# Retention and SwiGLU kernel: a second joined attention visit in two down-projections, and the loads placed to match

## The chip, the cores and the metric

The kernel runs on one core of one Trainium2 chip. The metric is the device time of one execution in microseconds (us). The engines named below are TensorE (PE, with its weight loads as PEld), VectorE (DVE), ScalarE (ACT), GpSimd (POOL) and SyncE (SP), which issues transfers.

## The reference

A retention layer (linear attention with a decaying state) feeds a feed-forward layer.

```python
# q, k, v: (batch 4, heads 8, seq 768, head_dim 64)
gamma = 1.0 - 2.0 ** (-5.0 - np.arange(H))
for t in range(S):
    state = gamma * state + einsum('bhd,bhe->bhde', k[:, :, t], v[:, :, t])
    y[:, :, t] = scale * einsum('bhd,bhde->bhe', q[:, :, t], state)
# x: y with its heads side by side, 3072 tokens x 512
xn = x / sqrt(mean(x * x) + 1e-6) * rms_g
out = (silu(xn @ w_gate) * (xn @ w_val)) @ w_out     # 512 -> 1536 -> 512
```

## The kernel before, in words

**Chunks and units.** The 768 positions are cut into six chunks of 128. A chunk holds four units, one for each batch; units 0 and 1 are pair 0, units 2 and 3 are pair 1, so a pair is 256 tokens and a chunk is 512. `(d, b)` below is unit `b` of chunk `d`; `(d, p)` after `values` or `a_pair` is a pair.

**Attention of a chunk.** `load` brings q, k and v of a unit from memory by three transfers that GpSimd issues (q and k are cast to bf16 on the way). `vp` scales v by the decay on GpSimd. `t_dma` transposes q and k into `qT` and `kT` by two transfers that SP issues. `a_pair` computes q-k products of a pair (`a_ps`, line 488): for each unit into two PSUM banks. `a_mask` (DVE, line 497) applies the causal mask and copies them out as `am`. `values` computes for a pair the products of `am` and `vp` (line 517), the k-v products for the state (`kv_ps`, line 526, not in the last chunk) and the product of `qT` and the old state `st_b` (line 534). `y_out` (DVE) scales the result into `x`, `state_add` (DVE) adds `kv_ps` to the state, `state_cast` (POOL) recasts it to bf16. Then `square` (ACT) and `rstd` (POOL) give the norm's factor, `norm` (DVE) writes `xn`, and `x_dma` (SP) transposes it into `xnT`, which `begin` has set up.

**Feed-forward of a chunk.** `gv` computes gate and value products of one or two of the twelve 128-column blocks of the hidden layer (lines 563, `g_ps` and `v_ps`), ACT applies silu (`sg`) and DVE multiplies (`hT`). `down` multiplies one unit's `hT` by `w_out` (line 584), ACT copies the result out (`o_sb`) and SP stores it. In the loop at the end of the kernel the first four `gv` steps of a chunk take 256 tokens and two blocks each, so the first two need pair 0 of `xnT` and the next two pair 1; eight steps with 512 tokens and one block follow.

**Order.** The order on every engine is the order of the program; nothing is moved by a scheduler. From chunk 1 on the feed-forward of chunk `c` is a list of 16 steps (0 to 11 `gv`, 12 to 15 `down`), and the attention of chunk `d = c + 1` is threaded between them: `after[n]` lists what is issued behind step `n`. In the loop at the end of the kernel `c` runs from 2 to 5. A stretch of attention work on TensorE between two steps is called a visit here.

A joined visit is a call such as `values(d, 1, (d + 1, 0), True)`: the values of pair 1 of chunk `d` are followed at once by the q-k products of pair 0 of the next chunk. The last argument puts the values' PSUM tiles into the banks of the feed-forward (four, taken in turn), while the q-k products take the other four. Before, each of the steps 11 of `c` = 2 and `c` = 3 (and no other) carries such a visit.

**Queues and buffers.** Transfers on one queue are issued in the program's order, and an issue that waits for its data holds up all that stand behind it on that engine: a `t_dma` on SP waits for its load to land, and `x_dma` and the stores of `down` share SP with it. On GpSimd the loads share the order with `vp`, `rstd` and `state_cast`. All transfers run on the same 16 DMA engines. There are six buffers for `v`, eight each for `q`, `k`, `qT`, `kT` and `vp`, and twelve for `am`.

Of the kernel before, what the change touches and what calls it, by code (L numbers as in the profile page):

```python
# [16 lines left out]
def kernel(  # L17
# [16 lines left out]
    NCH = S // C  # L34
# [716 lines left out]
    def run(steps, after):  # L751
        for i, step in enumerate(steps):
            MARK[i] = step()
            for f in after.get(i, ()):
                f()

    def L(f, *a):
        return lambda: f(*a)
# [20 lines left out]
        12: [L(values, 2, 1), L(load, 3, 2, "qkv", 12),  # L779
             L(y_out, 2, 1, 0), L(y_out, 2, 1, 1), L(square, 2, 1, 0), L(square, 2, 1, 1), L(rstd, 2, 1),  # L780
             L(state_add, 2, 1), L(norm, 2, 1, 0, 1), L(x_dma, 2, 1, 0), L(x_dma, 2, 1, 1),
             L(state_cast, 1), L(vp, 3, 0), L(load, 3, 3), L(vp, 3, 1), L(t_dma, 3, 2)],
        14: [L(t_dma, 3, 3)],
    })

    for c in range(2, NCH):

        steps = [L(gv, c, n, n + 2, t, t + 256) for t in (0, 256) for n in (0, 2)]
        steps += [L(gv, c, n, n + 1, 0, GT) for n in range(4, NFF)]
        steps += [L(down_last if (c, b) == (NCH - 1, B - 1) else down, c, b) for b in range(B)]  # L790
        d = c + 1
        more = d + 1 < NCH
        after = {}
        if d == 3:
            after = {
                0: [L(begin, d)],
                1: [L(a_pair, d, 0), L(a_mask, d, 0, 0)],
                2: [L(a_mask, d, 0, 1), L(a_mask, d, 1, 0)],
                3: [L(a_mask, d, 1, 1), L(load, d + 1, 0)],
                4: [L(values, d, 0), L(vp, d, 2), L(vp, d, 3)],  # L800
                5: [L(y_out, d, 0, 0), L(y_out, d, 0, 1), L(state_add, d, 0), L(load, d + 1, 1)],
                6: [L(square, d, 0, 0), L(square, d, 0, 1), L(rstd, d, 0), L(t_dma, d + 1, 0)],
                7: [L(a_pair, d, 1), L(a_mask, d, 2, 0), L(state_cast, 0)],
                8: [L(a_mask, d, 2, 1), L(a_mask, d, 3, 0), L(t_dma, d + 1, 1), L(vp, d + 1, 0), L(load, d + 1, 2)],
                9: [L(a_mask, d, 3, 1), L(norm, d, 0, 0), L(x_dma, d, 0, 0), L(vp, d + 1, 1)],
                10: [L(norm, d, 0, 1), L(x_dma, d, 0, 1), L(load, d + 1, 3)],
            }
        elif d < NCH:
            after = {
                0: [L(begin, d)],  # L810
                1: [L(values, d, 0)] + [L(load, d + 1, 0)] * more,
                2: [L(y_out, d, 0, 0), L(vp, d, 2), L(vp, d, 3)],
                3: [L(y_out, d, 0, 1)] + [L(state_add, d, 0), L(load, d + 1, 1)] * more,
                4: [L(square, d, 0, 0)],
                5: [L(a_pair, d, 1), L(a_mask, d, 2, 0), L(square, d, 0, 1), L(rstd, d, 0)]
                   + [L(state_cast, 0), L(t_dma, d + 1, 0)] * more,
                6: [L(t_dma, d + 1, 1), L(load, d + 1, 2)] * more + [L(a_mask, d, 2, 1), L(norm, d, 0, 0), L(x_dma, d, 0, 0)],
                7: [L(norm, d, 0, 1), L(x_dma, d, 0, 1), L(a_mask, d, 3, 0)] + [L(vp, d + 1, 0)] * more,
                8: [L(a_mask, d, 3, 1)] + [L(load, d + 1, 3), L(vp, d + 1, 1)] * more,
            }  # L820
        if d < NCH:
            if more:
                after.update({
                    11: [L(values, d, 1, (d + 1, 0), True), L(y_out, d, 1, 0), L(y_out, d, 1, 1),
                         L(square, d, 1, 0), L(square, d, 1, 1), L(rstd, d, 1), L(state_add, d, 1),
                         L(a_mask, d + 1, 0, 0), L(a_mask, d + 1, 0, 1), L(norm, d, 1, 0, 1), L(x_dma, d, 1, 0)],
                    12: [L(x_dma, d, 1, 1), L(a_mask, d + 1, 1, 0, 1), L(state_cast, 1), L(t_dma, d + 1, 2)],
                    13: [L(t_dma, d + 1, 3)],
                })
            else:  # L830
                after.update({
                    9: [L(values, d, 1)],
                    10: [L(y_out, d, 1, 0)],
                    11: [L(y_out, d, 1, 1), L(square, d, 1, 0), L(square, d, 1, 1), L(rstd, d, 1)],
                    12: [L(norm, d, 1, 0, 1), L(x_dma, d, 1, 0), L(x_dma, d, 1, 1)],
                })
        run(steps, after)
# [1 line left out]
_INS = ['q', 'k', 'v', 'moe_w_gate', 'moe_w_val', 'moe_w_out', 'moe_rms_g']  # L839
# [26 lines left out]
```

## Time and profile before

| | |
|---|---|
| median of 5 runs | 238.81 us (237.41 to 239.49) |
| the profiled execution: its own time | 240.91 us |
| its span, first to last instruction | 238.9 us |
| mean granted TensorE clock | 0.993 of full speed |
| busy: DVE, ACT, POOL | 127.1, 87.6, 118.3 us |
| gate and value products (line 563) | 76.0 and 75.8 us |
| down-projections (lines 584 and 598) | 61.1 and 2.8 us |
| loads and weights on GpSimd's queue | 17.04 MB, 72.6% of the DMA engines' time |
| SP's queue: transposes, stores | 13.25 MB, 33.5% of it |

The profile covers one execution. The busy time of an engine is the union of its instructions' spans; the mean duration of a single matmul is longer than its share of the busy time, because matmuls are pipelined. The two queues' shares add up to over 100% because packets of several queues overlap on an engine. The chain of waits follows the work that ended last back to what released it, step by step. In the lists in order of time, a row has start, length, engine, line, operation, and the number of instructions merged into it. A transfer's time to landing counts from its issue.

### The profile page before, as it was taken

To read this page: it belongs to the slowest core of one execution; us is meant where nothing else is said; L and a number is where in the kernel's file an instruction comes from. 1 tells how busy PE (TensorE), PEld (TensorE's weight loads), DVE (VectorE), ACT (ScalarE), POOL (GpSimd) and SP (SyncE) were. 2 spreads that over 40 slices of the span, in tenths; PEclk is the share of its full clock that TensorE was granted. 3 is DMA by queue.
4 is the path that set the end of the run, shared out by engine and by line. 5 is a ranking of instruction groups with operands and counts; after the bars stand their busy time and mean duration, and the time that the engine had idled before them with its cause. 6 is when DMAs were issued, how large, how long until landed. Compare 5 with 4: busy or idle time off the path is not lost.

```text
span 238.9 us, 5561 instructions
## 1 busy us (share of the span) xinstructions
PE 227.8 (95%) x2290; PEld 138.6 (58%) x2290; DVE 127.1 (53%) x222; ACT 87.6 (37%) x176; POOL 118.3 (50%) x154
## 2 busy tenths in 40 slices
PE   6887999999999999599999999999999999999994
PEld 2455775546888854485454585454684544864443
DVE  3775545826577784145798037868145842234300
ACT  2965634233432423122524225314235242333211
POOL 8966799589598839960595901937001001000000
PEclk9999999999999999889999999999999999999999
DMA  8999999999999999999999999891640204200022
GB/s 101 166 184 203 188 181 172 194 200 211 169 164 137 142 159 133 180 243 172 73 108 112 187 192 200 87 135 27 172 113 0 47 0 130 93 0 0 0 92 88
DMA packets 87467, 30.78 MB, mean 129 GB/s; under 512 B 73681, under 2 KB 83153, under 8 KB 87442
## 3 DMA queue, kind: packets, MB, share of 16 engines
q0 software_dynamic: 55488, 17.04, 72.6%
q1 hardware_dynamic: 31280, 13.25, 33.5%
q8 instruction: 18, 0.29, 0.6%
q10 hardware_dynamic: 674, 0.14, 0.3%
q14 instruction: 7, 0.06, 0.1%
HBM read 29.36 MB, written 6.29 MB: 149 GB/s over the span
## 4 chain that ended last, share of the span: by engine, by line
PE 82%; DMA 9%; DVE 4%; issue 2%; POOL 2%; DVEq 0%; POOLq 0%
PE g_ps L563 25%; PE v_ps L563 24%; PE o_ps L584 22%; DMA xnT<-xn 3%; DMA wv_b<-in_moe_w_val_dram 3%; DMA k2b<-in_k_dram 2%; PE a_ps L488 2%; PE y_ps L517 2%; DVE am L290 1%; PE y_ps L534 1%; PE o_ps L598 1%; PE kv_ps L526 1%; DVE hT L568 1%; PE a_ps L283 1%; DVE am L497 1%
## 5 line engine op out<-in xcount | busy, mean ns | idle before, releaser
L568 DVE TENSOR_TENSOR hT<-sg,v_ps 128x512 bf16<-128x512 bf16 (+1 forms) x76 | 49.9, 657 | 78.1 <-PE v_ps L563 74.4
L563 PE MATMUL g_ps<-xnT,wg_b 128*128 128x256 bf16 (+1 forms) x428 | 76.0, 313 | 3.4 <-DMA xnT<-xn 2.5
L563 PE MATMUL v_ps<-xnT,wv_b 128*128 128x256 bf16 (+1 forms) x428 | 75.8, 312 | 0.9 <-DMA wv_b<-in_moe_w_val_dram 0.7
L567 ACT ACTIVATE sg<-g_ps 128x512 bf16<-128x512 f32 (+1 forms) x76 | 43.7, 575 | 78.3 <-PE g_ps L563 78.1
L584 PE MATMUL o_ps<-wo_b,hT 128*128 128x512 bf16 x276 | 61.1, 379 | 0.0
L563 PEld LDWEIGHTS <-wv_b 128*128 128x128 bf16 x428 | 42.0, 99 | 22.8 <-DMA wv_b<-in_moe_w_val_dram 1.7
L563 PEld LDWEIGHTS <-wg_b 128*128 128x128 bf16 x428 | 40.7, 99 | 24.6 <-issue 3.6
L584 PEld LDWEIGHTS <-hT 128*128 128x128 bf16 x276 | 26.5, 98 | 31.4
L457 POOL TENSOR_SCALAR m<-ms 128x2 f32<-128x2 f32 x10 | 2.2, 218 | 61.9 <-ACT xsq L452 61.9
L588 ACT COPY o_sb<-o_ps 128x512 f32<-128x512 f32 x23 | 13.4, 584 | 43.7 <-PE o_ps L584 36.1
L465 DVE SCALAR_TENSOR_TENSOR xn<-x,rstd,g_bc 128x512 bf16<-128x512 f32 x20 | 19.2, 987 | 9.8 <-POOL rstd L373 9.8
L497 DVE TENSOR_TENSOR am<-a_ps,causal 128x512 bf16<-128x512 f32 x32 | 21.1, 681 | 0.0
L471 POOL TENSOR_TENSOR vp<-v_f,vd_n 128x512 bf16<-128x512 f32 x16 | 19.0, 1193 | 2.1 <-DMA v_f<-in_v_dram 2.1
L114 POOL DMA_DIRECT2D qb<-in_q_dram x18 | 17.0, 942 | 5.6 <-ACT o_sb L588 4.4
L114 POOL DMA_DIRECT2D kb<-in_k_dram x18 | 16.0, 891 | 2.0 <-DMA wo_b<-in_moe_w_out_dram 2.0
L452 ACT ACTIVATE xsq<-x 128x512 bf16<-128x512 f32 x20 | 12.4, 622 | 12.5 <-DVE x L443 10.1
L111 POOL DMA_DIRECT2D v_f<-in_v_dram x16 | 14.6, 912 | 0.0
L443 DVE TENSOR_TENSOR x<-y_ps,yd_n 128x512 f32<-128x512 f32 x16 | 10.5, 684 | 1.5 <-PE y_ps L534 1.3
L222 PE MATMUL hot<-ones 128*128 128x512 bf16 x28 | 8.8, 439 | 1.4 <-DVE ones L149 1.4
L303 POOL TENSOR_TENSOR vp<-v2f,vd_p 128x1024 bf16<-128x1024 f32 x4 | 7.7, 1932 | 0.1
L373 POOL TENSOR_TENSOR rstd<-m,mhalf 128x2 f32<-128x2 f32 x10 | 7.2, 720 | 0.8
L102 POOL DMA_DIRECT2D q2b<-in_q_dram x8 | 5.8, 738 | 0.8 <-POOLq L850 0.8
(96 smaller groups left out, 153.9 us busy)
## 6 DMA issues: line engine op xcount, KB each, us to landing
v_f<-in_v_dram POOLq DMA_DIRECT2D x16, 256.0 KB, 7.7
out_dram<-o_sb SPq DMA_DIRECT2D x15, 256.0 KB, 2.3
qb<-in_q_dram POOLq DMA_DIRECT2D x18, 128.0 KB, 6.7
kb<-in_k_dram POOLq DMA_DIRECT2D x18, 128.0 KB, 7.4
out_dram<-o_sb SPq DMA_DIRECT2D x17, 128.0 KB, 6.7
wg_b<-in_moe_w_gate_dram POOLq DMA_DIRECT2D x6, 256.0 KB, 7.9
wv_b<-in_moe_w_val_dram POOLq DMA_DIRECT2D x6, 256.0 KB, 8.5
wo_b<-in_moe_w_out_dram POOLq DMA_DIRECT2D x3, 512.0 KB, 10.1
```

The lines of the kernel that those rows point to most:

```text
L111: i = nc.gpsimd.dma_start(out=x, in_=unit_v[n][c, b])
L114: i = nc.gpsimd.dma_start(out=x.rearrange("p (h d) -> p h d", h=H), in_=unit_v[n][c, b])
L443: nc.vector.tensor_tensor(out=x[:, :, :, i, :], in0=u["y"][i].rearrange("p (b a d) -> p b a d", b=2, a=NHP), in1=yd_n[:, c, i][:, None, :, ...
L452: nc.scalar.activation(xsq, u["x"][:, b], AF.Square, scale=1.0 / math.sqrt(DM), accum_out=u["ms_"][:, b:b + 1])
L465: nc.vector.scalar_tensor_tensor(out=u["xn"][b], in0=u["x"][:, b], scalar=u["rstd"][:, b:b + 1], in1=g_bc, op0=ALU.mult, op1=ALU.mult)
L471: nc.gpsimd.tensor_tensor(out=x, in0=U[c, b]["v"], in1=vd_n[:, c, :, None].to_broadcast([128, H, D]), op=ALU.mult)
L497: nc.vector.tensor_tensor(out=x, in0=u["a_ps"][i].rearrange("p (a t) -> p a t", a=NHP), in1=causal[:, None, :].to_broadcast([128, NHP, 128 ...
L563: nc.tensor.matmul(x[:, o:o + w], wt[:, s, n * 128:(n + 1) * 128], XT[c][:, s, t0:t1], start=s == 0, stop=s == KS - 1)
L567: nc.scalar.activation(sg[:, :m], ps[0][:, :m], AF.Silu)
L568: return nc.vector.tensor_tensor(out=HT[c][:, n0:n1, t0:t1], in0=sg[:, :m].rearrange("p (n t) -> p n t", t=w), in1=ps[1][:, :m].rearrange( ...
L584: nc.tensor.matmul(ps, HT[c][:, n, b * C:(b + 1) * C], wo_b[:, n, :], start=n == 0, stop=n == NFF - 1)
L588: i = nc.scalar.copy(o_sb, ps)
```

## The change

For `c` = 2 and `c` = 3 (the third and fourth down-projection of the kernel) a second joined visit is put behind step 13, the second `down`: the values of pair 0 of the next chunk, already with its k-v products and state, followed by the q-k products of its pair 1. Their visits in the next chunk's `gv` steps go. What remains of that pair's work there (`square`, `rstd`, `norm`, `x_dma`) moves to its steps 0 to 3. For the last chunk pair 1's values come behind step 1 of `c` = 4, instead of step 9, and what follows from them moves forward with them.

The loads and transposes are moved so that all four units of the next chunk are there: with `c` = 2, loads 2 and 3 of chunk 4 go to steps 6 and 8 (from 8 and 10), `t_dma` of its units 2 and 3 to steps 10 and 11 (from 12 and 13), and their `vp` from the next chunk's step 2 to step 12. On SP the four transposes now stand ahead of `x_dma` of chunk 3's pair 1. On GpSimd load 2 stands ahead of the state's recast and of `vp` of unit 0. With `c` = 3 the loads of chunk 5 are issued behind steps 1, 3, 5 and 7, each transposed and scaled three steps later; on GpSimd they now stand behind `rstd` of chunk 4's pair 0. In the schedule of chunk 1's feed-forward, load 3 of chunk 3 moves behind `vp` of unit 1.

```diff
--- before.py
+++ after.py
@@ -779,7 +779,7 @@
         12: [L(values, 2, 1), L(load, 3, 2, "qkv", 12),
              L(y_out, 2, 1, 0), L(y_out, 2, 1, 1), L(square, 2, 1, 0), L(square, 2, 1, 1), L(rstd, 2, 1),
              L(state_add, 2, 1), L(norm, 2, 1, 0, 1), L(x_dma, 2, 1, 0), L(x_dma, 2, 1, 1),
-             L(state_cast, 1), L(vp, 3, 0), L(load, 3, 3), L(vp, 3, 1), L(t_dma, 3, 2)],
+             L(state_cast, 1), L(vp, 3, 0), L(vp, 3, 1), L(load, 3, 3), L(t_dma, 3, 2)],
         14: [L(t_dma, 3, 3)],
     })
 
@@ -796,44 +796,49 @@
                 0: [L(begin, d)],
                 1: [L(a_pair, d, 0), L(a_mask, d, 0, 0)],
                 2: [L(a_mask, d, 0, 1), L(a_mask, d, 1, 0)],
-                3: [L(a_mask, d, 1, 1), L(load, d + 1, 0)],
+                3: [L(a_mask, d, 1, 1), L(load, 4, 0)],
                 4: [L(values, d, 0), L(vp, d, 2), L(vp, d, 3)],
-                5: [L(y_out, d, 0, 0), L(y_out, d, 0, 1), L(state_add, d, 0), L(load, d + 1, 1)],
-                6: [L(square, d, 0, 0), L(square, d, 0, 1), L(rstd, d, 0), L(t_dma, d + 1, 0)],
+                5: [L(y_out, d, 0, 0), L(y_out, d, 0, 1), L(state_add, d, 0), L(load, 4, 1)],
+                6: [L(square, d, 0, 0), L(square, d, 0, 1), L(rstd, d, 0), L(t_dma, 4, 0), L(load, 4, 2)],
                 7: [L(a_pair, d, 1), L(a_mask, d, 2, 0), L(state_cast, 0)],
-                8: [L(a_mask, d, 2, 1), L(a_mask, d, 3, 0), L(t_dma, d + 1, 1), L(vp, d + 1, 0), L(load, d + 1, 2)],
-                9: [L(a_mask, d, 3, 1), L(norm, d, 0, 0), L(x_dma, d, 0, 0), L(vp, d + 1, 1)],
-                10: [L(norm, d, 0, 1), L(x_dma, d, 0, 1), L(load, d + 1, 3)],
+                8: [L(a_mask, d, 2, 1), L(a_mask, d, 3, 0), L(t_dma, 4, 1), L(vp, 4, 0), L(load, 4, 3)],
+                9: [L(a_mask, d, 3, 1), L(norm, d, 0, 0), L(x_dma, d, 0, 0), L(vp, 4, 1)],
+                10: [L(norm, d, 0, 1), L(x_dma, d, 0, 1), L(t_dma, 4, 2)],
+                11: [L(t_dma, 4, 3)],
             }
         elif d < NCH:
             after = {
-                0: [L(begin, d)],
-                1: [L(values, d, 0)] + [L(load, d + 1, 0)] * more,
-                2: [L(y_out, d, 0, 0), L(vp, d, 2), L(vp, d, 3)],
-                3: [L(y_out, d, 0, 1)] + [L(state_add, d, 0), L(load, d + 1, 1)] * more,
-                4: [L(square, d, 0, 0)],
-                5: [L(a_pair, d, 1), L(a_mask, d, 2, 0), L(square, d, 0, 1), L(rstd, d, 0)]
-                   + [L(state_cast, 0), L(t_dma, d + 1, 0)] * more,
-                6: [L(t_dma, d + 1, 1), L(load, d + 1, 2)] * more + [L(a_mask, d, 2, 1), L(norm, d, 0, 0), L(x_dma, d, 0, 0)],
-                7: [L(norm, d, 0, 1), L(x_dma, d, 0, 1), L(a_mask, d, 3, 0)] + [L(vp, d + 1, 0)] * more,
-                8: [L(a_mask, d, 3, 1)] + [L(load, d + 1, 3), L(vp, d + 1, 1)] * more,
+                0: [L(square, d, 0, 0), L(square, d, 0, 1), L(rstd, d, 0)],
+                2: [L(norm, d, 0, 0)],
+                3: [L(norm, d, 0, 1), L(x_dma, d, 0, 0), L(x_dma, d, 0, 1)],
             }
-        if d < NCH:
             if more:
-                after.update({
-                    11: [L(values, d, 1, (d + 1, 0), True), L(y_out, d, 1, 0), L(y_out, d, 1, 1),
-                         L(square, d, 1, 0), L(square, d, 1, 1), L(rstd, d, 1), L(state_add, d, 1),
-                         L(a_mask, d + 1, 0, 0), L(a_mask, d + 1, 0, 1), L(norm, d, 1, 0, 1), L(x_dma, d, 1, 0)],
-                    12: [L(x_dma, d, 1, 1), L(a_mask, d + 1, 1, 0, 1), L(state_cast, 1), L(t_dma, d + 1, 2)],
-                    13: [L(t_dma, d + 1, 3)],
-                })
+                for j, (n, t) in enumerate(((1, 4), (3, 6), (5, 8), (7, 10))):
+                    after.setdefault(n, []).append(L(load, d + 1, j))
+                    after.setdefault(t, []).extend([L(t_dma, d + 1, j), L(vp, d + 1, j)])
             else:
                 after.update({
-                    9: [L(values, d, 1)],
-                    10: [L(y_out, d, 1, 0)],
-                    11: [L(y_out, d, 1, 1), L(square, d, 1, 0), L(square, d, 1, 1), L(rstd, d, 1)],
-                    12: [L(norm, d, 1, 0, 1), L(x_dma, d, 1, 0), L(x_dma, d, 1, 1)],
+                    1: [L(values, d, 1)],
+                    4: [L(y_out, d, 1, 0)],
+                    5: [L(y_out, d, 1, 1), L(square, d, 1, 0), L(square, d, 1, 1), L(rstd, d, 1)],
+                    7: [L(norm, d, 1, 0), L(x_dma, d, 1, 0)],
+                    8: [L(norm, d, 1, 1), L(x_dma, d, 1, 1)],
                 })
+        if more:
+
+            e = d + 1
+            after.setdefault(11, []).extend([
+                L(values, d, 1, (e, 0), True), L(y_out, d, 1, 0), L(y_out, d, 1, 1), L(state_add, d, 1),
+                L(square, d, 1, 0), L(square, d, 1, 1), L(rstd, d, 1),
+                L(a_mask, e, 0, 0, 1), L(a_mask, e, 1, 0, 1), L(norm, d, 1, 0), L(x_dma, d, 1, 0)])
+            after.update({
+                12: [L(norm, d, 1, 1), L(x_dma, d, 1, 1), L(state_cast, 1)]
+                    + ([L(vp, e, 2), L(vp, e, 3)] if d == 3 else []),
+                13: [L(begin, e), L(values, e, 0, (e, 1), True), L(y_out, e, 0, 0), L(y_out, e, 0, 1)]
+                    + [L(state_add, e, 0), L(state_cast, 0)] * (e + 1 < NCH)
+                    + [L(a_mask, e, 2, 0, 1), L(a_mask, e, 3, 0)],
+                14: [L(a_mask, e, 3, 1)],
+            })
         run(steps, after)
 # ---- launch: one core; inputs and outputs as the reference has them ----
 _INS = ['q', 'k', 'v', 'moe_w_gate', 'moe_w_val', 'moe_w_out', 'moe_rms_g']
```

## Prediction

> **What bounds the kernel now.** I read the page's busy times first, then the chain of waits in order of time, then the clock and the queues in the stretches that the edit touches. TensorE is busy for 95% of the span:
>
> ```profile
> PE 227.8 (95%) x2290; PEld 138.6 (58%) x2290; DVE 127.1 (53%) x222; ACT 87.6 (37%) x176; POOL 118.3 (50%) x154
> ```
>
> The chain of waits (start, length, what) says where TensorE's time goes:
>
> ```profile
> 89.96 8.29 DMA xnT<-xn
> 98.39 1.03 PE g_ps L563 x8
> ...
> 139.42 0.47 PE y_ps L517 x16
> ...
> 140.60 0.98 PE g_ps L563 x8
> 141.58 0.87 PE v_ps L563 x8
> ...
> 147.65 0.55 PE a_ps L488 x16
> 148.21 0.97 PE g_ps L563 x4
> ...
> 158.67 0.47 PE y_ps L517 x16
> ...
> 160.29 10.47 PE o_ps L584 x48
> ```
>
> Up to 98.39 TensorE waits for a transposed input of chunk 2. From there to the end the chain is TensorE almost without a gap, gate and value products, down-projections and short visits to the attention. A visit's price is therefore read directly: its own length, plus about 0.11 us by which the first group behind it is longer (0.98 against 0.87). The busy times by stretch (length, PE, PEld, DVE, ACT, POOL, then granted clock) show what the wait before 98.39 cost besides itself:
>
> ```profile
> 95.90:98.40 2.50, 0.03 (x2) 0.04 (x2) 0.00 (x0) 0.00 (x0) 2.50 (x3) 1.00 2.33 161
> 98.40:103.70 5.30, 5.30 (x34) 3.87 (x36) 0.69 (x1) 1.68 (x3) 4.06 (x6) 0.68 1.74 191
> ```
>
> After 2.47 us idle the clock fell to a mean of 0.68, and four half groups took 5.32 us where four such groups take 3.49 (4 x 0.87): 1.83 us more. The whole event is 4.30 us.
>
> Last the queues where the new visit takes its inputs. GpSimd, in order of time:
>
> ```profile
> 116.42 0.72 POOL L373 TENSOR_TENSOR rstd<-m,mhalf 128x2 f32<-128x2 f32 x1
> 117.10 0.60 POOL L351 CAST st_b<-st_f 128x512 bf16<-128x512 f32 x1
> 117.67 1.03 POOL L471 TENSOR_TENSOR vp<-v_f,vd_n 128x512 bf16<-128x512 f32 x1
> 118.66 0.99 POOL L114 DMA_DIRECT2D qb<-in_q_dram  x1
> ...
> 122.41 0.94 POOL L114 DMA_DIRECT2D qb<-in_q_dram  x1
> 123.35 0.89 POOL L114 DMA_DIRECT2D kb<-in_k_dram  x1
> ```
>
> These are chunk 4's loads 2 and 3. Two transposes on SP, by tile, with the time to landing:
>
> ```profile
> L546 SPq DMA_TRANSPOSE xnT<-xn x1: 1295/1295/1295, 124.4 to 124.4; - x1
> DMA to landing us min/median/max: 8.7/8.7/8.7
> ```
> ```profile
> L479 SPq DMA_TRANSPOSE kT<-kb x1: 1282/1282/1282, 145.8 to 145.8; - x1
> DMA to landing us min/median/max: 3.4/3.4/3.4
> ```
>
> The first ran beside loads and took 8.7 us; the second was the last of four in a row with no load beside it and took 3.4. Others beside loads: 5.1 (issued at 152.2), 5.6 (154.1), 5.9 (kT at 138.7); on quiet rings 2.4 to 2.5 (164.9, 169.4).
>
> **The change, part by part.** Both built programs list 4579 rows on TensorE: no arithmetic goes or comes.
>
> *Visits.* A values visit alone costs 1.18 (139.42 to 140.60) + 0.11 = 1.29 us, a q-k visit alone 0.55 + 0.11 = 0.66; together 1.95. Joined they cost 1.62 (158.67 to 160.29) + 0.11 (10.47 against 10.36 for four undisturbed down-projections at 194.05) = 1.73. The change makes one such pair joined in chunk 2's down-projection: 0.22 us less. In chunk 3's the last chunk has no k-v products (0.37 us): apart 0.81 (174.25 to 175.06) + 0.11 + 0.66 = 1.58, joined 1.73 - 0.37 = 1.36, again 0.22. Sum: -0.44 us, on TensorE, thus on the path.
>
> *The new wait.* The visit after chunk 2's second down-projection needs kT of chunk 4's units 2 and 3, which so far were read first at 147.65. When does it ask? The joined visit ends at 125.46 and two down-projections take 0.11 + 10.36/2, so 130.75; the values take 1.18, half the q-k products 0.22: kT of unit 3 must be there at 132.15. When does it come? Load 2 goes straight behind rstd, at 117.14, the state cast and vp after it: 2.76 (118.66 to 121.42) brings it to 119.9, cast 0.60 and vp 1.03 to 121.5, q 0.94, so k of load 3 is issued at 122.45, only 0.9 us earlier than before. It lands 5.0 (the k load issued at 119.65) to 8.2 us (123.35) later, 127.5 to 130.7. On SP the two xnT issues end at 125.73 (124.44 + 1.29); four transposes of 1.27 follow, so the last is issued at 129.5 if its k has landed, as it mostly has. Landing: 131.9 by the 2.4 us row, 132.9 by 3.4, 135.4 by 5.9, 138.2 by 8.7. The wait is 0, 0.75, 3.25 or 6.05 us. Load 3's v, issued near 123.4, lands 5.7 to 8.9 us later (rows of 155.22 and 124.21), 129.1 to 132.3, so the transposes run beside a load for part of their time, between the 3.4 and the 5.9 row; I take the middle, 4.6: landing 134.1, wait 1.95 us. Behind it on TensorE stand two down-projections and all of chunk 3: nothing else can run, and it is paid in full.
>
> The Trainium skill ("DMA: Bandwidth & Descriptors", section "Queues, rings and completion order") says each DMA engine alternates, packet by packet, between the rings that hold work, which speaks against issuing four transposes beside a load. Worked from that and the quiet 2.4 us, a transpose beside one load would take about 4.8 us, an estimate, and the wait would be 2.15; the rows beside loads are longer, 5.1 to 8.7.
>
> *Clock.* A wait of 2.47 us cost 1.83 more (above); pauses of 0.66 and 0.73 us at 20.15 and 21.50 left the clock at 1.00. For 1.95 us I take 0 and keep 1.83 for the range. The Trainium skill's "TensorE: Matmul & The Clock Gate", section "Why this matters for your kernels", forbids idle gaps over about 3 us only; by it no wait here up to 3 us costs more than itself, while the 2.47 us row says that one can.
>
> *What else the visit needs* is covered: VectorE reads x, state and masks from 125.05 (1.29, 0.68, 1.28 in the rows, two masks more at 1.2) and is done at 129.3, 1.4 us early; vp and the recast state come by 125.2, before 130.75 and 131.6. Its PSUM banks are those of the first visit and the first down-projection, copied out by 128.8. If VectorE were late by those 1.4 us, the excess would be added.
>
> *SP's other work.* Chunk 3's second pair of xnT goes behind the four transposes: 130.03 becomes 130.8, 131.95 becomes 132.7. Landing in 7.4 us (the row of 131.95) gives 140.1; the reader, the third group of chunk 3, starts at 135.93 + 1.73 + 1.95 + 3.49 = 143.1. Cost 0, cover 3.0. The store of the first down-projection moves from 131.33 to about 132.1, lands by 136.8 (4.7), before the fourth down-projection's copy at 139.6: 0.
>
> *Chunk 3's second visit.* Chunk 5's loads now start behind rstd of chunk 4, some 3.2 us into chunk 3 (142.8), and each vp between them waits for its v (5.0 to 8.9 us). That puts the last k at 155.4 to 159.3, landed 160.4 to 167.5, transposed 162.8 to 170.9. TensorE asks at 168.4. I take 0 and keep 2.5 us.
>
> *Load 3 of chunk 3* is issued behind one vp (1.07 us) later, at 94.94. It may take traffic away from the xnT that TensorE awaits until 98.39, but that one was issued at 89.96 with other loads beside it. From 0 to all 4.30 us of that event; I take 0. Its own transposes were issued at 101.60 and 102.95, its data landing at 101.50 plus 1.1: no loss.
>
> *Sum.* -0.44 + 1.95 = +1.5 us. The profiled execution took 240.91 us (span 238.9), 2.1 more than the median of 238.81; much of that may be the 4.30 us event. The difference goes onto the median: 240.3 us.
>
> **The rivals.** *In time:* the four transposes land by the 3.4 us row or sooner. For it: no load follows chunk 4's now, so rings empty after about 131. Against it: rings paused in this very place before (8.7). It gives -0.44 to +0.3, 238.4 to 239.1; the forecast is slower only when the last kT takes over 4.3 us. This is the case that is not slower. *The early wait shrinks:* if the later load frees the rings before 98, up to 4.30 us go on the profiled run, on the median at most 4.30 - 2.1 = 2.2. Half of this with transposes in time gives 238.81 - 0.44 - 1.1 = 237.3. Against it: that load was issued when 3.9 of the 8.29 us were over. *Wait and clock:* 5.1 to 5.9 us landings with the clock's 1.83 give -0.44 + 2.85 + 1.83 = +4.2, 243.0.
>
> **How the numbers follow.** A difference under 0.5%, 1.2 us, can't be told from none here. Forecast, with waits from 1.6 to 3.3 us and full clock: 0.36. Wait and clock, or chunk 3's second visit late as well: 0.11. In time: 0.30, all within 0.5%. Early wait shrinks: 0.23, of it 0.20 beyond 0.5%. So faster 0.20, same 0.33, slower 0.47. The range leaves out some 0.08 at the bottom and 0.09 at the top: 237.3 to 242.4; the forecast's own is 240.0 to 241.7.
>
> **What would show it.** A wait of a_ps for kT near 132 in chunk 2's down-projection, about 2 us and the only new one, with kT issued near 129.5; joined visits of 1.62 and 1.25 us; chunk 3's twelve groups with no visit among them; xnT of chunk 3 ahead of its reader. I am wrong if that wait is under 0.5 us, if the clock falls near 135, if kT of chunk 5 is late, or if TensorE no longer idles before 98.

## The result and the profile after

The changed kernel is slower by a third of a per cent: its median is 239.94 us (237.57 to 244.78, 35 runs) against 238.81 us (237.15 to 241.71, 59 runs), the ratio 1.0035 with a 95% interval of 1.0014 to 1.0055. The ratio leaves disturbed runs out, so it gives 0.8 us (0.3 to 1.3) where the medians give 1.1. The forecast was 240.3 us, +1.5. The measured difference is under the 0.5% that the prediction took as the line between slower and same. The profiled execution of the changed kernel took 242.13 us, with a span of 240.2 us and a clock of 0.998.

The busy times of the page show no change that matters; TensorE still does the same 2290 matmul records in 95% of the span:

```profile
PE 227.5 (95%) x2290; PEld 138.4 (58%) x2290; DVE 126.1 (52%) x222; ACT 87.4 (36%) x176; POOL 118.7 (49%) x154
```

The chain of waits of the changed kernel (start, length, what):

```profile
93.47 6.49 DMA xnT<-xn
...
100.09 1.03 PE g_ps L563 x8
...
125.28 5.30 PE o_ps L584 x24
...
130.78 2.50 DMA kT<-kb
...
133.33 0.40 PE a_ps L488 x8
133.72 5.29 PE o_ps L584 x24
...
167.97 5.29 PE o_ps L584 x24
```

Behind the second down-projection, which ends at 130.58, the chain leaves TensorE for one transfer: kT, issued at 130.78 and landed 2.50 us later. This is the predicted wait, at the predicted place. Chunk 3's second visit, which ends at 167.97, has none. TensorE in order of time (start, length, line, operation, idle before and releaser) shows the wait in two pieces, one for each of the two transposes that came late:

```profile
132.16 0.40 PE L488 MATMUL a_ps<-qT,kT 64*128 64x128 bf16 x8 [0.42 <-DMA kT<-kb]
133.33 0.40 PE L488 MATMUL a_ps<-qT,kT 64*128 64x128 bf16 x8 [0.77 <-DMA kT<-kb]
```

The first of the two is kT of unit 2, issued at 127.22 and landed after 4.9 us. The visit took 133.72 - 130.58 = 3.14 us where an undisturbed one takes 1.62, so the wait costs 1.52 us. The two idle times add up to only 1.19: the two halves of the q-k products take 0.40 us each, where the chain of `mid` (below) has 0.45 for all 16 in an undisturbed visit. The stretch behind it (length, PE, PEld, DVE, ACT, POOL, clock) kept a clock of 1.00, so nothing was added to the wait here:

```profile
133.70:139.00 5.30, 5.30 (x28) 2.44 (x27) 2.35 (x4) 0.59 (x1) 0.61 (x1) 1.00 0.59 184
```

SP in order of time says why that kT was late:

```profile
127.22 1.20 SPq L479 DMA_TRANSPOSE kT<-kb  x1
128.52 2.17 SPq L479 DMA_TRANSPOSE qT<-qb  x1
130.78 1.23 SPq L479 DMA_TRANSPOSE kT<-kb  x1
```

The last of the four transposes is the row at 130.78. The issue ahead of it took 2.17 us where the others took 1.2, and why is not shown. It was no accident of one execution: in `again` the same issue took 2.43 us, in `nowait` that of the last kT took 2.52. Chunk 3's second pair of xnT follows at 132.10 and 134.05; it landed at 134.56 and 136.47, well ahead of its reader at 142.51.

**A measure that leaves the start out.** Single executions differ most before chunk 2: in the profiles below, the first group of chunk 2 starts between 95.6 and 102.6 us, and edits that stand behind that point cannot have made this spread of 7 us. I therefore compare lengths from the first gate group of a chunk to that of the next, read from TensorE in order of time. A swap of two lines in the kernel before (`swap`, below) gave an execution with that order and no wait inside these chunks.

| us, first group to first group | chunk 2 | chunk 3 | chunk 4 | sum |
|---|---|---|---|---|
| before (clock fell in chunk 2) | 37.37 | 34.84 | 33.64 | 105.85 |
| `swap`: the old order, undisturbed | 35.72 | 34.83 | 33.65 | 104.20 |
| after | 38.76 | 34.25 | 32.14 | 105.15 |
| `again`: after, a second time | 38.91 | 34.25 | 32.13 | 105.29 |
| `mid`: the new order, no wait for kT here | 37.38 | 34.24 | 32.14 | 103.76 |
| `one`: a second joined visit in chunk 3 only | 35.71 | 36.21 | 32.13 | 104.05 |

From the first group of chunk 5 to TensorE's end all take 31.35 or 31.36. Chunks 3 and 4 repeat to 0.02 us, so the table measures tenths where the times of whole runs can't.

### The profile page after: what moved, and what is told of

Same layout as the page of the kernel before. It is cut to its first block, busy times and chain, and to the rows that moved or that the text cites. A ratio compares the mean times of both kernels' runs of the same rounds, so it can differ in the third digit from the quotient of the medians.

```text
span 240.2 us, 5567 instructions
## 1 busy us (share of the span) xinstructions
PE 227.5 (95%) x2290; PEld 138.4 (58%) x2290; DVE 126.1 (52%) x222; ACT 87.4 (36%) x176; POOL 118.7 (49%) x154
## 4 chain that ended last, share of the span: by engine, by line
PE 77%; DMA 14%; DVE 3%; POOL 3%; issue 1%; ACT 0%; SPq 0%; POOLq 0%; DVEq 0%
PE g_ps L563 23%; PE v_ps L563 23%; PE o_ps L584 22%; DMA wv_b<-in_moe_w_val_dram 5%; DMA kT<-kb 4%; DMA xnT<-xn 3%; DMA v2f<-in_v_dram 2%; PE a_ps L488 2%; PE y_ps L517 1%; PE o_ps L598 1%; PE y_ps L534 1%; POOL q2b L102 1%; PE kv_ps L526 1%; POOL wg_b L86 1%; DVE hT L568 1%
## 5 line engine op out<-in xcount | busy, mean ns | idle before, releaser
L563 PE MATMUL v_ps<-xnT,wv_b 128*128 128x256 bf16 (+1 forms) x428 | 75.0, 309 | 2.5 <-DMA wv_b<-in_moe_w_val_dram 2.4
L563 PE MATMUL g_ps<-xnT,wg_b 128*128 128x256 bf16 (+1 forms) x428 | 75.1, 310 | 2.3 <-DMA xnT<-xn 1.6
L465 DVE SCALAR_TENSOR_TENSOR xn<-x,rstd,g_bc 128x512 bf16<-128x512 f32 x20 | 17.8, 911 | 6.2 <-POOL rstd L373 6.2
L497 DVE TENSOR_TENSOR am<-a_ps,causal 128x512 bf16<-128x512 f32 x32 | 20.4, 680 | 0.0
L222 PE MATMUL hot<-ones 128*128 128x512 bf16 x28 | 10.0, 490 | 1.4 <-DVE ones L149 1.4
L488 PE MATMUL a_ps<-qT,kT 64*128 64x128 bf16 x128 | 5.3, 217 | 2.1 <-DMA kT<-kb 2.1
```

What stands on the lines that cost most here:

```text
L465: nc.vector.scalar_tensor_tensor(out=u["xn"][b], in0=u["x"][:, b], scalar=u["rstd"][:, b:b + 1], in1=g_bc, op0=ALU.mult, op1=ALU.mult)
L497: nc.vector.tensor_tensor(out=x, in0=u["a_ps"][i].rearrange("p (a t) -> p a t", a=NHP), in1=causal[:, None, :].to_broadcast([128, NHP, 128 ...
L563: nc.tensor.matmul(x[:, o:o + w], wt[:, s, n * 128:(n + 1) * 128], XT[c][:, s, t0:t1], start=s == 0, stop=s == KS - 1)
```

## The experiments

Theory A: the wait for kT in the new visit costs in full and outweighs what the joins save. Theory B: the difference is made in the first 100 us by the later load 3 of chunk 3, and the new wait takes little or nothing. Each edit is to the changed kernel unless it says otherwise.

**`nowait`: the wait's reader takes other data.** For chunk 4 the q-k products of units 2 and 3 read the transposes of units 0 and 1, which are long there. Every transfer stays where it is.

```diff
+        s = U[c, b - 2] if c == 4 and b > 1 else u
...
-                nc.tensor.matmul(..., u["kT"][r, hp, :], u["qT"][r, hp, :],
+                nc.tensor.matmul(..., s["kT"][r, hp, :], s["qT"][r, hp, :],
```

> The changed kernel with every transfer in its place, but the q-k products of chunk 4's pair 1 read qT and kT of units 0 and 1, which landed 10 us earlier, so that part of the computation is changed (only the data, not the work). Theory A (the wait for kT in chunk 2's down-projection, and the clock that it sometimes takes down, is the whole loss): second visit 1.62 us, chunk 2 takes 37.1 us from its first group to that of chunk 3, about 238.4 us, ratio 0.998, and as many runs with a full clock as the kernel before (24 of 29), where the changed kernel had 21 of 35. Theory B (the loss lies elsewhere, in transfers or in the first 100 us): ratio stays at 1.003 or more.

It ran at 0.9953 of before (0.9909 to 0.9998), the changed kernel `again` on the same chip at 1.0020 (0.9976 to 1.0063). Its chain, whose line numbers stand one higher:

```profile
130.90 0.47 PE y_ps L518 x16
...
132.52 5.29 PE o_ps L585 x24
```

The second visit, from 130.90 to 132.52, takes 1.62 us, the undisturbed length. With the wait gone and all transfers in place the loss is gone too: for A. The two ratios differ by 0.67%, 1.6 us, about the 1.52 of the wait. But the two intervals overlap, so this pair alone would not be enough, and the kernel came out further below the kernel before than the missing wait explains. In its profile the first visit waited 0.42 us for a kT, so chunk 2 took 37.81 us, not the 37.1 expected. The clock does not tell the two apart: its mean was below 0.995 in 3 of 12 runs here and in 2 of 12 of `again`.

**`again`: the changed kernel once more**, as the partner of the runs on this chip.

> The changed kernel itself, on the same chip and against the same runs of the kernel before: ratio 1.002 to 1.008, a wait for kT of 0.5 to 2.5 us in chunk 2's second visit.

1.0020 (0.9976 to 1.0063), median 239.66. The wait stood again at the same place, 0.58 and 0.52 us, and chunk 2 was as long as in the first profile (38.91).

**`late`: the wait made longer.** The transposes of unit 3 go behind chunk 3's second pair of xnT.

```diff
-                11: [L(t_dma, 4, 3)],
...
-                    + ([L(vp, e, 2), L(vp, e, 3)] if d == 3 else []),
+                    + ([L(t_dma, 4, 3), L(vp, e, 2), L(vp, e, 3)] if d == 3 else []),
```

> The changed kernel, but the two transposes of unit 3 of chunk 4 stand behind both xnT of chunk 3's pair 1 on SP. Theory A: kT is issued near 135.4 instead of 130.78 and lands 2.5 us later, so the wait grows from 1.5 to about 6 us and the time by 4.5 us, ratio 1.022; if the clock falls behind this wait, 1.8 us more, 1.030. Theory B (such waits are made good later, the first 100 us decide): ratio under 1.010.

1.0257 (1.0188 to 1.0327; 4 runs), median 244.76. TensorE in order of time:

```profile
127.93 0.40 PE L488 MATMUL a_ps<-qT,kT 64*128 64x128 bf16 x8 [0.59 <-DMA kT<-kb]
132.45 0.50 PE L488 MATMUL a_ps<-qT,kT 64*128 64x128 bf16 x8 [4.12 <-DMA kT<-kb]
```

Idle for 4.71 us instead of 1.19, and the two down-projections behind it took 6.89 us instead of 5.35, since the clock fell. Chunk 2 grew to 43.92, 5.2 us more than after, and the run by about as much: 2.2% more in ratio is 5.3 us. A wait in this place is paid in full, as A says, and this one cost 1.54 us more behind it by the clock.

**`load33`: the load move of chunk 3 undone.**

```diff
-             L(state_cast, 1), L(vp, 3, 0), L(vp, 3, 1), L(load, 3, 3), L(t_dma, 3, 2)],
+             L(state_cast, 1), L(vp, 3, 0), L(load, 3, 3), L(vp, 3, 1), L(t_dma, 3, 2)],
```

> The changed kernel, but load 3 of chunk 3 is issued ahead of vp of unit 1 again, as in the kernel before. Theory A: nothing changes, ratio 1.003 to 1.005 and a wait for kT of about 1.5 us in the second visit. Theory B: the ratio falls to 1.000 or less.

1.0065 (1.0022 to 1.0107), median 241.03: with the old place of the load the kernel is not faster, so B falls. The wait for kT stood again, and here it pulled the clock down. TensorE in order of time, then the stretch behind it, with a clock of 0.76 (the number behind POOL's); the two down-projections in it took 7.04 us instead of 5.35:

```profile
129.47 0.40 PE L488 MATMUL a_ps<-qT,kT 64*128 64x128 bf16 x8 [1.15 <-DMA kT<-kb]
130.39 0.40 PE L488 MATMUL a_ps<-qT,kT 64*128 64x128 bf16 x8 [0.52 <-DMA kT<-kb]
```
```profile
130.70:137.80 7.10, 7.10 (x30) 2.98 (x27) 1.94 (x4) 0.58 (x1) 0.29 (x1) 0.76 0.43 135
```

**`swap`: the load move alone.** The kernel before, with only the order of that one line changed.

```diff
-             L(state_cast, 1), L(vp, 3, 0), L(load, 3, 3), L(vp, 3, 1), L(t_dma, 3, 2)],
+             L(state_cast, 1), L(vp, 3, 0), L(vp, 3, 1), L(load, 3, 3), L(t_dma, 3, 2)],
```

> The kernel before with one line of the change alone: load 3 of chunk 3 behind vp of unit 1. Theory C (this move shortens the wait for xnT ahead of chunk 2 and spares the fall of the clock behind it; it is why the run one came out at 0.996 where 0.999 was expected): ratio 0.994 to 0.997, a full clock in nearly all runs, where the kernel before had 21 of 35 in the last comparison. Theory A alone (the move does nothing): 1.000, the clock as before.

0.9978 (0.9945 to 1.0012), median 237.81: no loss from the move, perhaps a small gain, but the interval includes none. The idle before chunk 2 is still there (2.04 us in its profile), so the later load does not remove it. Theory C asked for a full clock in nearly all runs; it was below 0.995 in 3 of 12, against 9 of 35 of the kernel before on that chip, which shows no such effect.

**`early`: loads 2 and 3 of chunk 4 sooner.**

```diff
-                5: [..., L(load, 4, 1)],
-                6: [..., L(t_dma, 4, 0), L(load, 4, 2)],
+                5: [..., L(load, 4, 1), L(load, 4, 2), L(load, 4, 3)],
+                6: [..., L(t_dma, 4, 0)],
...
-                8: [..., L(t_dma, 4, 1), L(vp, 4, 0), L(load, 4, 3)],
+                8: [..., L(t_dma, 4, 1), L(vp, 4, 0), L(t_dma, 4, 2)],
...
-                10: [..., L(t_dma, 4, 2)],
+                10: [...],
```

> The changed kernel, but loads 2 and 3 of chunk 4 are issued right behind load 1 (step 5), in GpSimd's idle time before rstd, and their transposes stand at steps 8 and 11. Theory A (the new wait for kT outweighs the 0.44 us of the joined visits): the second visit of chunk 2's down-projection is 1.62 us long without a wait (3.14 in the changed kernel), and the time is about 1.5 us below the changed kernel, 238.4 us or a ratio of 0.998 to the kernel before. Theory B (the loss comes from the first 100 us, where load 3 of chunk 3 was moved and TensorE reached chunk 2 at 100.09 instead of 98.39): the wait goes all the same, but the ratio stays near 1.0035.

1.0010 (0.9976 to 1.0043). The wait in the second visit is gone, and a new one stands in the first: the transposes of unit 1 now run beside two loads. By tile, the kT of unit 1 in this kernel:

```profile
L479 SPq DMA_TRANSPOSE kT<-kb x1: 2167/2167/2167, 113.1 to 113.1; - x1
...
DMA to landing us min/median/max: 9.9/9.9/9.9
```

and the same transpose in the changed kernel:

```profile
L479 SPq DMA_TRANSPOSE kT<-kb x1: 1697/1697/1697, 116.6 to 116.6; - x1
...
DMA to landing us min/median/max: 4.6/4.6/4.6
```

It took 9.9 us instead of 4.6, and TensorE idled 0.51 us for it at 122.5. The ratio lies between the forecasts of A (0.998) and B (1.0035) and decides nothing.

**`early_t31`: `early`, with unit 1's transposes of chunk 3 moved on SP** behind chunk 2's xnT that they stood ahead of.

```diff
-             L(rstd, 2, 0), L(t_dma, 3, 1)],
-        11: [..., L(x_dma, 2, 0, 0), L(x_dma, 2, 0, 1)],
+             L(rstd, 2, 0)],
+        11: [..., L(x_dma, 2, 0, 0), L(x_dma, 2, 0, 1),
+             L(t_dma, 3, 1)],
```

> As early, and besides the two transposes of unit 1 of chunk 3 go behind the two xnT of chunk 2's pair 0 on SP, which wait there for nothing but their place. xnT should be issued about 1.6 us sooner after its norm. Theory A with that: TensorE's wait for xnT ahead of chunk 2 (2.47 us before, 1.59 in the changed kernel) falls under 0.7 us, and the ratio to the kernel before is 0.990 to 0.994. If traffic and not the place on SP sets that landing, the ratio is that of early, 0.998.

1.0047 (1.0009 to 1.0085). The first visit waited 1.77 us, more than in `early`; nothing was gained. TensorE did not idle ahead of chunk 2 in its profile, but neither did it in that of `early`, so what the place on SP does stays open.

**`mid`: one load less in the way.** Load 2 at step 5, load 3 at step 6 behind `rstd`, `t_dma(4, 2)` at step 8.

```diff
-                5: [..., L(load, 4, 1)],
-                6: [..., L(t_dma, 4, 0), L(load, 4, 2)],
+                5: [..., L(load, 4, 1), L(load, 4, 2)],
+                6: [..., L(t_dma, 4, 0), L(load, 4, 3)],
...
-                8: [..., L(t_dma, 4, 1), L(vp, 4, 0), L(load, 4, 3)],
+                8: [..., L(t_dma, 4, 1), L(vp, 4, 0), L(t_dma, 4, 2)],
...
-                10: [..., L(t_dma, 4, 2)],
+                10: [...],
```

> The changed kernel, but load 2 of chunk 4 is issued behind load 1 and load 3 behind rstd, so only one load more stands beside the transposes of units 0 and 1 (two in the run early, where the first visit waited for kT of unit 1). Transposes of unit 2 go ahead of xnT of pair 0. Theory A: neither visit waits over 0.3 us, about 238.4 us, ratio 0.998. If one load is still too many, the first visit waits 0.3 to 1 us, ratio 1.000 to 1.003.

Its profile shows what was hoped for, both visits undisturbed, the second in 1.62 us:

```profile
130.13 0.47 PE y_ps L517 x16
...
131.75 5.29 PE o_ps L584 x24
```

And yet it ran at 1.0035 (0.9989 to 1.0081), median 240.32: A's 0.998 lies just outside this interval, and taken alone these whole runs speak against A. The clock does not explain it. In 5 of the 12 runs its mean was below 0.995, about one fall, but the kernel before had 14 of 35 such runs on the same chip. The profiled execution idled 2.04 us for a kT at 73.4, in code that all these kernels share. Whether its other executions waited in chunk 2 after all stays open.

**`one`: the second joined visit in chunk 3 only.** Chunk 2's stage and the stage of chunk 3 up to the joined visit are as in the kernel before; load 3 of chunk 3 stays moved, and chunk 5's transposes of units 2 and 3 go to steps 10 and 11.

```diff
-                6: [..., L(t_dma, 4, 0), L(load, 4, 2)],
+                6: [..., L(t_dma, 4, 0)],
...
-                8: [..., L(load, 4, 3)],
+                8: [..., L(load, 4, 2)],
...
-                10: [..., L(t_dma, 4, 2)],
-                11: [L(t_dma, 4, 3)],
+                10: [..., L(load, 4, 3)],
+                11: [L(values, d, 1, (4, 0), True), ...],
+                12: [..., L(t_dma, 4, 2)],
+                13: [L(t_dma, 4, 3)],
+            }
+        elif d == 4:
+            after = {...
+                10: [L(t_dma, 5, 2), L(vp, 5, 2)],
+                11: [L(t_dma, 5, 3), L(vp, 5, 3)],
...
-        if more:
+        if d == 4:
```

> Chunk 2's down-projection and chunk 3's first pair as in the kernel before; the second joined visit in chunk 3's down-projection alone. Theory A: chunk 2 takes 35.5 us, chunks 3 and 4 together 0.22 us less than before, no wait of TensorE behind 100 us: ratio 0.999, not to be told from 1. Theory B (chunk 3's part loses too): over 1.002.

0.9960 (0.9925 to 0.9996), median 237.53 (236.32 to 238.37). In its profile TensorE has no idle time over 0.3 us behind 26 us, and the joined visit of chunk 3 finds its kT there. None of its 12 runs had a mean clock below 0.995, where the kernel before had 14 of 35 on this chip.

**`one_2`: `one` again**, on another chip.

> The run one once more, on this chip: 0.995 to 0.998 if its gain is real, 0.999 to 1.000 if it was the scatter of the kernel before.

0.9980 (0.9944 to 1.0017), median 238.10. Both runs of `one` lie below 1, the second with an interval that includes it. It is the lowest of the three versions: 0.2 to 0.4% below the kernel before, and below the changed kernel `again` on the first chip (0.9960 against 1.0020), though these two intervals overlap. The added join explains little of it: by the table above the sum is 0.15 us shorter than in `swap` (104.05 against 104.20), 0.06%. The full clock of all runs of `one` did not come again: 4 of 12 runs of `one_2` were below 0.995, against 9 of 35 of the kernel before.

**`one_l33`: `one` with load 3 of chunk 3 at its old place** (the line of `load33`).

> The run one with load 3 of chunk 3 back ahead of vp of unit 1. Theory C: the ratio rises to 0.998 to 1.000 and part of the runs lose clock again. Theory A alone: 0.996 as in one.

0.9995 (0.9960 to 1.0030) beside `one_2` at 0.9980, a difference that the intervals do not separate. The profile shows what the move does. In this kernel a wait stands inside chunk 2, for xnT of its pair 1; the chain:

```profile
95.27 6.22 DMA xnT<-xn
...
101.63 1.03 PE g_ps L563 x8
```

and `one`, in which the same transpose landed 4.4 us after its issue and the group behind the visit starts without a gap:

```profile
99.24 0.55 PE a_ps L488 x16
99.79 0.98 PE g_ps L563 x8
```

TensorE idles 0.89 us here in `one_l33` (chunk 2 takes 36.68 instead of 35.71) and 0.80 in `load33`, the two kernels with the old place of the load that did not idle ahead of chunk 2. None of the seven profiles with the new place and no idle there shows one of over 0.2 us. So by these profiles, two against seven, the moved load spares about 0.9 us in executions that did not already lose it ahead of chunk 2.

**`one_t31`: `one` with the SP order of `early_t31`.**

> The run one, and the two transposes of unit 1 of chunk 3 behind the xnT of chunk 2's pair 0. If the place on SP still delays xnT in some runs, 0.5 to 1 us less than one (0.993); if one has no wait left ahead of chunk 2, the same as one.

0.9990 (0.9950 to 1.0030): nothing gained.

## Why the prediction was right, and where its terms were off

The direction, the place and the mechanism held: a wait of TensorE for the last kT of chunk 4 between chunk 2's second and third down-projection, larger than what the joins save. The lengths between fixed instructions show that it decides: over chunks 2 to 4 the changed kernel takes 105.15 us with the wait, `mid` 103.76 without it, the old order 104.20. On whole runs `late` shows it and `nowait` agrees, while those of `mid` do not. The size is right in part by luck: errors inside one term partly cancelled, and terms that the sum left out made up for others. By the prediction's own line of 0.5% the outcome is its "same" (0.33), not its "slower" (0.47), and 239.94 lies just below the forecast's own 240.0 to 241.7. By its steps:

**Visits, -0.44.** Chunk 3 got shorter by 34.83 - 34.25 = 0.58 and chunk 4 by 33.65 - 32.14 = 1.51. Chunk 2 without its wait is 38.76 - 1.52 = 37.24 against 35.72, 1.52 longer, 0.57 us less than the other two gave. Of this the joins made only 0.35: in chunk 2's first joined visit the values products of line 517 took 0.63 us in the changed kernel and 0.85 before and in `swap`, by TensorE in order of time. The traces show where these 0.22 went. The chain of the kernel before passes from an `hT` of VectorE to these products:

```profile
122.98 0.68 DVE hT L568
123.71 0.60 PE y_ps L517 x15
```

The products take banks of the feed-forward, and that `hT` reads one of them. It is late because the `norm` ahead of it on VectorE takes 1.22 us while GpSimd's `vp` of unit 1 runs beside it (first two rows, before). In the changed kernel load 2 and the state's recast have other places, `vp` is done when the `norm` starts, and the `norm` takes 0.74 (last two rows):

```profile
121.42 1.07 POOL L471 TENSOR_TENSOR vp<-v_f,vd_n 128x512 bf16<-128x512 f32 x1
121.84 1.22 DVE L465 SCALAR_TENSOR_TENSOR xn<-x,rstd,g_bc 128x512 bf16<-128x512 f32 x1
```
```profile
120.40 1.06 POOL L471 TENSOR_TENSOR vp<-v_f,vd_n 128x512 bf16<-128x512 f32 x1
121.89 0.74 DVE L465 SCALAR_TENSOR_TENSOR xn<-x,rstd,g_bc 128x512 bf16<-128x512 f32 x1
```

In all 14 profiles this `norm` takes 1.14 to 1.23 us with a `vp` beside it (seven) and 0.74 without (seven). So this reordering on GpSimd, whose effect on VectorE the prediction did not price, gave 0.22 us beside the 0.35 of the joins. The added visit itself thus cost 1.74, the 1.73 of the prediction; the last chunk's visits gave 0.07 less than taken (1.51 for 1.58).

**The new wait, 1.95: the term that was mis-sized.** It measured 1.52 us, and both halves were off. The last kT was issued at 130.78, not 129.5: of four transposes taken at 1.27 us each, one took 2.17. The kernel before already had such issues on SP, of 1.58, 1.68 and 1.87 us (issued at 133.30, 136.92 and 143.82), the last in the very row of four that the prediction read for its 3.4 us:

```profile
143.82 1.87 SPq L479 DMA_TRANSPOSE qT<-qb  x1
```

The last kT landed after 2.50 us, not after the 4.6 taken as the middle between the 3.4 and 5.9 rows: load 3's v was in at 130.6, so no load ran beside it, as the rival "in time" had argued. The errors of 1.3 later and 2.1 sooner partly cancelled. The wait of 0.42 us for unit 2's kT was not in the working at all, which asked only for the last kT. The Trainium skill's rule that was weighed ("DMA: Bandwidth & Descriptors", "Queues, rings and completion order") gives 4.8 us beside one load, as an estimate. The unit 1 transpose beside one load took 4.6, which agrees, and beside two 9.9, four times the quiet 2.5 us. All loads stand on GpSimd's one queue, so turns between rings alone would give 4.8 there too, and the measurement decides.

**Clock, 0.** Right in the profile of the changed kernel (1.00 behind the wait), wrong in `load33`, where a wait of the same kind (1.15 + 0.52 us idle) was followed by a fall, as was the longer one of `late`. The mean clock was below 0.995 in 14 of 35 runs of the changed kernel, in 2 of 12 of `again`, and in 28 of 99 of the kernel before: that the change adds falls is possible, not shown.

**What was costed at nothing.** xnT of chunk 3 landed ahead of its reader; the store moved and was not missed; chunk 3's second visit asked for its kT at 167.7, issued at 162.56, and did not wait (0, as taken, of the 2.5 us kept). Load 3 of chunk 3 was taken at 0 and is worth up to -0.9 us, as `one_l33` shows, in those executions that do not idle ahead of chunk 2.

**What the sum lacked.** The last step of the program. The chain of the kernel before ends like this, after TensorE's end at 235.61:

```profile
235.65 0.04 issue
235.69 0.42 DVE o_sb L225
```

and the chain of the changed kernel, after TensorE's end at 236.60:

```profile
236.64 0.40 issue
237.03 0.42 DVE o_sb L225
```

VectorE copies the last result 0.36 us later. This stands in all eight profiles of kernels with the second joined visit in chunk 2 and in none of the other six. What the copy waited for last is, by the profile, the last products (line 598) in the eight, and a store of `o_sb` in the six. Why this differs was not tried, and the cause stays open. With it the profiles add up to -0.57 + 1.52 + 0.36 = +1.3 us, the upper end of the measured 0.3 to 1.3; the moved load lowers it in some executions.

**The rivals.** "In time" named the landing rightly (2.50 us) and the issue wrongly. "The early wait shrinks" is not settled: TensorE still idled 1.59 us ahead of chunk 2, and 2.04 in `swap`, but the wait comes and goes from one execution to the next, in 4 of 11 profiles with the new place of the load and in 1 of 3 with the old. "Wait and clock" happened in `load33`.

## What to carry to other kernels

Two joined visits save a few tenths of a microsecond, and one input that came late in them cost 1.5 us, so ask of each merged step when its last operand is issued and what is queued ahead of it on that queue. Where the cover is missing, bringing loads forward may only move the wait to the transposes that now share the rings; merging only where the operand is far ahead (`one`) left no wait, for a gain of 0.15 us between fixed instructions. When the start of a program varies by more than the effect, measure lengths between fixed instructions behind it.

## What was not expected of the hardware

The clock does not fall by the length of a pause alone. It fell behind 1.15 + 0.52 us of idle time (`load33`), behind 1.80 (`swap`, at 22.7), 2.04 (`mid`, at 73.4), 2.47 (before) and 4.12 (`late`), each time for 3.4 us at half speed (in `load33` a granted clock of 0.50 from 131.4 to 134.8), and not behind 1.77 (`early_t31`), 1.78 (`one_l33`, at 22.0), 2.04 ahead of chunk 2 (`swap`) or 0.42 + 0.77 (after). The Trainium skill's "TensorE: Matmul & The Clock Gate", section "Why this matters for your kernels", asks for no gaps over about 3 us; here pauses from 1.7 us on were already at risk, and the measurement decides.

Two other surprises are told above: a `norm` on VectorE takes 1.22 us instead of 0.74 beside a `vp` on GpSimd, and VectorE starts its last copy 0.36 us late.
